# A planned attention, mix and channel kernel: gating reads removed, loads planned at another rate and later into freed buffers, one PV cost changed

## The chip, the cores and the metric

The kernel runs on one core of a Trainium2 chip. The metric is the device time of one execution in microseconds. Before the change the median of three runs is 783.98 us (780.27 to 784.87). The profile is one further execution, which took 784.69 us; its span, from the first to the last instruction, is 782.9 us.

## The reference

Three blocks follow each other, all in float32, for a batch of 4, 8 heads of 64, a sequence of 576 and a model width of 512.

```python
scores = scale * np.matmul(q, k.transpose(0, 1, 3, 2))
mask_plain = (rel >= 0) & (rel < window)                      # heads 0 to 3, window 32
mask_dil = (rel >= 0) & (rel < window * dilation) & (rel % dilation == 0)   # heads 4 to 7, dilation 4
attn = softmax(np.where(mask, scores, -1e9)); out = attn @ v

xk = mu_k * x + (1.0 - mu_k) * x_prev
xr = mu_r * x + (1.0 - mu_r) * x_prev
k = np.maximum(xk @ w_k, 0.0)
v = k * k @ w_v
r = 1.0 / (1.0 + np.exp(-(xr @ w_r)))
x = r * v

h = xt @ U @ V
u = x + h.transpose(0, 2, 1)
ch = np.maximum(u @ w_ch1, 0.0) @ w_ch2
out = u + ch
```

The weights of the second and third block reach the device as 64-bit words and are turned into float32 there.

## The kernel before

**The work.** The sequence is cut into eight half batches of 288 positions, called chunks. Attention is done for units of one pair of heads in one part of a batch; `attend` does one unit, `attend2` two units in one visit. A visit is, in order: QK products (L676, L597 for single units), masking with a row minimum on VectorE (L537, called the masks here), exponentials on ScalarE (L546), sums inverted on VectorE (L551, L552), normalisation on GpSimd (L557), transposes (L714, L628), a copy of them to SBUF on ScalarE (`pts`, L352), PV products (L732, L640). A later visit's QK stands right behind an earlier visit's PV (`join`).

Each chunk is mixed with its shifted self (`mix`, L769) and multiplied with the weights in four receptance tiles, eight key tiles and four value tiles of two parts each. Chunk 0 uses exact float32 products (L828 for the receptance rows, L812 for keys and values). The chunks 1 to 7 use two-part operands with three products (L815, L816, L817), a set of three being called a trip here. Then come the channel products in five groups (L1036 to L1038, L1113 to L1115), until the end of the kernel.

**The weights.** A piece of 512 columns of the second block's weights is loaded into one of four buffers `w64` (`cv_load`, L368), and converted by ScalarE's absolute value (L385) and four VectorE instructions (L386, L387, L389, L392) to a piece `wx`. There are 20 such pieces, w0 to w19 in this text: w0 to w3 are for the receptance rows, w4 to w7 for key tiles 0 to 3, w8 to w11 for key tiles 4 to 7, w12 to w15 for the first parts of the values, w16 to w19 for their second parts. The value tiles' first parts and second parts take 16 products each by the listing, 32 matmuls in the trace. From chunk 1 on, each `wx` is divided into two parts (L352 and L349). The third block's weights go the same way, 32 pieces, through a DRAM copy (`w2f`, L419) that is read from chunk 7 on. Attention inputs come into four buffers `raw` (L526, L530, L534).

**What sets the order.** No engine chooses at run time. Each instruction is recorded by `op` with a duration from a cost formula; `plan` runs a model of the five engines ten times (`forward`, `backward`), keeps the shortest result, and its order is the order in which each engine executes. Engines are in order, so an instruction that waits holds all that stand behind it. For SyncE, which issues every DMA, the model takes 415 ns of issue, 1300 ns, the bytes at `RATE` one transfer after another, and 700 ns. A tile that takes a buffer from an earlier one may start 40 ns after the last use that the model sees.

**The gates.** From the fifth load to the twenty-eighth, `load` records before each load a DMA of four bytes from the tile of the load four places earlier to a scratch row in DRAM (L337). It waits for that earlier load, and SyncE waits with it. There are 24. A further limit stands in the built program: DMAs take turns on eight completion semaphores, and an issue waits until the DMA eight places earlier has landed.

Of the kernel before, what the change touches and what calls it, by code (L numbers as in the profile page):

```python
# [9 lines left out]
I32 = mybir.dt.int32  # L10
# [4 lines left out]
B, H, S, D = 4, 8, 576, 64  # L15
DM, DFF, DCH, RANK = 512, 1024, 2048, 32
P = 128
# [8 lines left out]
QW, KW = 32, 64  # L26
# [5 lines left out]
NALL = len(SETS)  # L32


def unit_kind(pair, part):

    if part == 0:
        if pair < 2:
            return 10, 320, (0,) + tuple(range(0, 288, 32)), (0, 1, 1)
        return 10, 320, tuple(0 if w == 0 else 160 if w == 5 else 32 * w - 32 for w in range(10)), (2, 3, 4)  # L40
    if pair < 2:
        return 8, 288, tuple(range(0, 256, 32)), (1, 1)
    return 8, 384, tuple(96 * (w // 2) + 32 * (w % 2) for w in range(8)), (1, 1)
# [9 lines left out]
QKW, VW = 640, 640  # L53
# [13 lines left out]
SLACK = 100.0  # L67
SLACK_PE = 100.0

OUTSTANDING = 4  # L70
GATED = 28
PLAN_PRINT = None
PASSES = 10
RATE = 245.0


@with_exitstack
def tile_attention_mix_channel(
    ctx: ExitStack, tc: tile.TileContext, qk0, qk1a, qk1b, v0, v0p, v1p, cst, mu, w1raw, w2raw, upk, vpk, out
):  # L80
    nc = tc.nc
# [7 lines left out]
    cst_t = cp.tile([P, P + NALL * KW], F32, name="cst_t")  # L89
    ident = cst_t[:, 0:P]  # L90
    masks = [cst_t[:, P + i * KW : P + (i + 1) * KW] for i in range(NALL)]
    mu_t = cp.tile([P, 8], F32, name="mu_t")
# [7 lines left out]
    ops = []  # L100
# [14 lines left out]
    def bank(tag):  # L115

        return Lazy([P, 512], F32, tag, f"ps{tag}", 4, ps)
# [4 lines left out]
    def op(eng, ns, fn, r=(), w=(), more=100, lock=False, mode=None, size=0):  # L122

        o = Op()
        o.eng, o.ns, o.fn, o.r, o.w, o.more, o.lock, o.mode, o.size = eng, ns, fn, list(r), list(w), more, lock, mode, size
        ops.append(o)

    def plan():
# [28 lines left out]
        def x_end(x):  # L157
            if x.end is not None:
                return x.end
            end = 0.0  # L160
            for u in reversed(x.ops):
                if u.done is None:
                    return NEVER
                end = max(end, u.done)
            x.end = end
            return end

        def ready(o):
            t = 0.0
            for d in o.deps:  # L170
                if d.done is None:
                    return None
                t = max(t, d.done + 40)
            if getattr(o, "behind", None) and o.behind.done is None:
                return None
            for x in o.tiles:
                if x.ops[0] is not o and x.ops[0].done is None:
                    return None
            for x in o.first:
                if x.at and x.line[x.at - 1].ops[0].done is None and x.line[x.at - 1].ops[0] is not o:  # L180
                    return None
                ends = sorted((x_end(y) for y in x.line[: x.at]), reverse=True)
                if len(ends) >= x.bufs:
                    if ends[x.bufs - 1] == NEVER:
                        return None
                    t = max(t, ends[x.bufs - 1] + 40)
            return t

        def forward(rank):
# [12 lines left out]
            while len(order) < len(ops):  # L202
# [3 lines left out]
                for e, q in queues.items():  # L206
                    pick = None
                    near = []
                    for o in q:
                        if o.i > low + WINDOW:  # L210
                            break
                        near.append(o)
                    if rank is not None and e != "SP":
                        near.sort(key=lambda o: rank[o.i])
                    for o in near:
                        t = ready(o)
                        if t is None:
                            continue
                        t = max(t, free[e])
                        if o.lock:  # L220
                            t = max(t, held["POOL" if e == "DVE" else "DVE"])
                        if o.mode and mode[e] != o.mode:
                            t += 90 if e == "PE" else 1283
                        if pick is None or t < pick[0] - (SLACK_PE if e == "PE" else SLACK):
                            pick = (t, o)
                        if t <= free[e]:
                            break
                    if pick and (best is None or pick[0] < best[0]):
                        best = pick
# [5 lines left out]
                if e == "SP":  # L235
                    begin = max(t + 1300, dma)
                    dma = begin + o.size / RATE
                    o.done = dma + 700
# [46 lines left out]
    def pe(ns, fn, r, w, mode, more=300):  # L285
        if joined is not None:
            joined.append((ns, fn, r, w, mode))
            return
        op("PE", ns, fn, r, w, more, mode=mode)
# [34 lines left out]
    def dma(nbytes, fn, r, w):  # L324
        op("SP", 415, fn, r, w, size=nbytes)

    landing = []
    gate_d = tc.dram_tile([1, 64], I32, name="gate_d")

    def load(nbytes, fn, key, at):  # L330

        k = len(landing)
        landing.append((key, at))
        gate = None
        if OUTSTANDING <= k < GATED:
            seen, where = landing[k - OUTSTANDING]
            op("SP", 415, lambda: nc.sync.dma_start(gate_d[:, k : k + 1], where().bitcast(I32)[0:1, 0:1]),  # L337
               [seen], [("gate", k)], size=4)
            gate = ops[-1]
        dma(nbytes, fn, [], [key])  # L340
        ops[-1].behind = gate

    def sub(eng, n, out_, a, b, r, w, psum=False, fr=True):

# [20 lines left out]

    def cv_load(src, n):
        raw = Lazy([P, CW], I64, "w64", "w64", 4)
        load(P * n * 8, lambda: nc.sync.dma_start(raw()[:, :n], src), (raw,), lambda: raw())  # L368
        return raw

    def cv_bits(raw, n, xt_=None):
# [135 lines left out]
    def unit(u):  # L507
        part_i, pair = divmod(u, NPAIR)
        b, part = divmod(part_i, 2)
        return b, part, pair  # L510

    def a_load(u, which=("qk", "v")):
        b, part, pair = unit(u)
        nw, kc = unit_kind(pair, part)[:2]
        src = qk0[b * NPAIR + pair] if part == 0 else (qk1a if pair < 2 else qk1b)[b * 2 + pair % 2]
        alone = u < NPAIR
        at_ = 0 if alone else pair % 2 * QKW

        def tile_of(key):
            if key not in raws:  # L520
                raws[key] = Lazy([P, 2 * QKW], F32, "raw", "raw", 4)
            return raws[key]

        if "qk" in which:
            raw = tile_of(u if alone else ("qk", u // 2))
            load(P * 4 * (nw * QW + kc), lambda: nc.sync.dma_start(raw()[:, at_ : at_ + nw * QW + kc], src),  # L526
                 (raw, at_), lambda: raw()[:, at_:])
        if "v" in which and alone:
            rv = tile_of(u)
            load(P * 4 * nw * D, lambda: nc.sync.dma_start(rv()[:, QKW : QKW + nw * D], v0[u]), (rv, "v"), lambda: rv()[:, QKW:])  # L530
        elif "v" in which and pair % 2:
            vt = tile_of(("v", u // 2))
            vsrc = v0p[(b - 1) * 2 + pair // 2] if part == 0 else v1p[b * 2 + pair // 2]
            load(P * 8 * nw * D, lambda: nc.sync.dma_start(vt()[:, : 2 * nw * D], vsrc), (vt, "v"), lambda: vt())  # L534

    def low(sc, c, pr, d, mk, mn, i, r=slice(0, P)):
        nc.vector.tensor_tensor_reduce(  # L537
# [112 lines left out]
    def attend2(ua, ub):  # L650
# [5 lines left out]
        nw, kc, starts, mk = unit_kind(pair, part)  # L656
        rq, rv = raws.pop(("qk", ua // 2)), raws.pop(("v", ua // 2))
# [4 lines left out]
        pt, ov = bank("S"), [bank("S") for _ in range(2)]  # L662
        pts = Lazy([P, 5 * P], F32, "pt", "pts", 2)
# [70 lines left out]
                            rhs=pts()[r, c : c + QW], start=True, stop=True,  # L734
                        )

        pe(nw * 4 * 30, pv, [(pts, k) for k in range(nw // 2 - 3)] + [(rv, "v")], [(x,) for x in ov], "pv")
        yield
        for x in range(2):
            x_out(ov[x], pair + x, part, b)  # L740
# [420 lines left out]
    def convert_to(n):  # L1161
        nonlocal converted
        while converted < min(n, len(jobs)):
            while len(loaded) < min(converted + AHEAD, len(jobs)):
                src, k, _ = jobs[len(loaded)]
                loaded.append(cv_load(src, k))
            jobs[converted][2](loaded[converted])
            converted += 1

    def next_piece():  # L1170
        src, k, _ = jobs[len(loaded)]
        loaded.append(cv_load(src, k))

    a_load(0, ["qk"])
    load(P * 4 * (P + NALL * KW), lambda: nc.sync.dma_start(cst_t, cst), ("cst",), lambda: cst_t)
    next_piece()
    a_load(0, ["v"])
    load(P * 32, lambda: nc.sync.dma_start(mu_t, mu), ("mu",), lambda: mu_t)
    a_load(1, ["qk"])
    next_piece()  # L1180
    a_load(1, ["v"])
# [70 lines left out]
    for j in range(3):  # L1252
        at_ = (0, 5, 12)[j]
# [140 lines left out]
```

## Time and profile before

| | |
|---|---|
| median of three runs | 783.98 us |
| the profiled execution, its time | 784.69 us |
| its span | 782.9 us |
| PE busy | 740.2 us, 95% |
| PE weight loads busy | 677.0 us, 86% |
| DVE busy | 563.9 us, 72% |
| ACT, POOL busy | 394.8 us, 386.1 us |
| DMA, mean | 140 GB/s, 41.8% of 16 engines' time on the one data queue |

PE is TensorE's matmul queue, DVE VectorE, ACT ScalarE, POOL GpSimd, SP SyncE. Matmuls are pipelined, so the sum of their durations exceeds the busy time. The granted clock is 1.00 at TensorE's full 2.4 GHz. The time of the execution is 1.8 us longer than its span.

### The profile page before, as it was taken

To read this page: it belongs to the slowest core of one execution; us is meant where nothing else is said; L and a number is where in the kernel's file an instruction comes from. 1 tells how busy PE (TensorE), PEld (TensorE's weight loads), DVE (VectorE), ACT (ScalarE), POOL (GpSimd) and SP (SyncE) were. 2 spreads that over 40 slices of the span, in tenths; PEclk is the share of its full clock that TensorE was granted. 3 is DMA by queue.
4 is the path that set the end of the run, shared out by engine and by line. 5 is a ranking of instruction groups with operands and counts; after the bars stand their busy time and mean duration, and the time that the engine had idled before them with its cause. 6 is when DMAs were issued, how large, how long until landed. Compare 5 with 4: busy or idle time off the path is not lost.

```text
span 782.9 us, 18285 instructions
## 1 busy us (share of the span) xinstructions
PE 740.2 (95%) x6866; PEld 677.0 (86%) x6866; DVE 563.9 (72%) x1334; ACT 394.8 (50%) x995; POOL 386.1 (49%) x408
## 2 busy tenths in 40 slices
PE   4876998999999999999998999999999999999998
PEld 3654798899899999998998899889888999889986
DVE  4869899999989853556466879766697965665632
ACT  4567578475867674554344535443444344334310
POOL 2223225355745554436377657644587754445600
PEclk9989999999999999999999999999999999999999
DMA  7865666766785512235662244123341411132001
GB/s 247 289 207 183 199 204 199 247 224 231 236 267 175 176 45 70 91 116 167 208 207 82 87 149 164 48 81 113 131 140 55 136 53 64 47 109 81 28 1 54
DMA packets 53273, 109.78 MB, mean 140 GB/s; under 512 B 5697, under 2 KB 15937, under 8 KB 53185
## 3 DMA queue, kind: packets, MB, share of 16 engines
q1 hardware_dynamic: 53184, 108.62, 41.8%
q8 instruction: 54, 0.88, 0.5%
q14 instruction: 35, 0.28, 0.1%
HBM read 86.05 MB, written 22.54 MB: 139 GB/s over the span
## 4 chain that ended last, share of the span: by engine, by line
PE 73%; DVE 13%; DMA 4%; issue 3%; ACT 3%; POOL 2%; SPq 0%; DVEq 0%; POOLq 0%; ACTq 0%
PE psS L1115 8%; PE psS L1113 8%; PE psS L1114 8%; PE psM L1036 7%; PE psM L1038 7%; PE psM L1037 7%; PE psM L815 7%; PE psM L816 6%; PE psM L817 6%; PE psS L732 2%; PE psS L676 1%; PE psM L812 1%; DVE pr L537 1%; DVE sums L472 1%; PE psM L828 1%
## 5 line engine op out<-in xcount | busy, mean ns | idle before, releaser
L347 POOL TENSOR_TENSOR cl<-sums,ch 128x512 fp32r<-128x512 f32 x72 | 98.3, 1366 | 89.2 <-ACT ch L352 60.0
L1115 PE MATMUL psS<-hl,rh 128*128 128x512 f32 (+1 forms) x320 | 119.8, 375 | 1.6 <-DVE hl L1051 1.6
L1113 PE MATMUL psS<-hh,rh 128*128 128x512 f32 (+1 forms) x320 | 119.3, 373 | 0.9 <-ACT hh L1050 0.5
L1114 PE MATMUL psS<-hh,rl 128*128 128x512 f32 (+1 forms) x320 | 119.1, 372 | 0.9 <-DVE rl L349 0.9
L352 ACT ACTIVATE ch<-sums 128x512 fp32r<-128x512 f32 (+1 forms) x104 | 57.3, 561 | 102.9 <-DVE sums L472 95.3
L815 PE MATMUL psM<-xk,wh 128*128 128x288 f32 x336 | 101.9, 303 | 0.0
L816 PE MATMUL psM<-xk,wl 128*128 128x288 f32 x336 | 99.8, 297 | 0.2 <-DVE wl L349 0.2
L817 PE MATMUL psM<-xk,wh 128*128 128x288 f32 x336 | 99.4, 296 | 0.0
L347 POOL TENSOR_TENSOR cl<-st,ch 128x256 fp32r<-128x256 f32 x80 | 65.5, 836 | 56.0 <-PE psM L1038 32.3
L472 DVE TENSOR_TENSOR sums<-st 128x256 f32<-128x256 f32 (+1 forms) x144 | 86.5, 651 | 5.0 <-POOL cl L347 3.8
L347 POOL TENSOR_TENSOR k2s<-k,k2s 128x288 fp32r<-128x288 f32 x49 | 46.5, 948 | 58.1 <-ACT k2s L352 56.3
L1115 PEld LDWEIGHTS psS<-hl,rh 128*128 128x128 f32 x320 | 60.5, 189 | 13.6 <-DVE hl L1051 2.0
L1113 PEld LDWEIGHTS psS<-hh,rh 128*128 128x128 f32 x320 | 60.5, 189 | 11.2 <-ACT hh L1092 1.2
L1114 PEld LDWEIGHTS psS<-hh,rl 128*128 128x128 f32 x320 | 60.5, 189 | 10.6 <-DVE rl L349 1.1
L347 POOL TENSOR_TENSOR xk<-m,xk 128x288 fp32r<-128x288 f32 x56 | 51.7, 936 | 36.2 <-ACT xk L352 30.5
L815 PE MATMUL psM<-k2s,wh 128*128 128x288 f32 x224 | 67.1, 300 | 0.0
L816 PE MATMUL psM<-k2s,wl 128*128 128x288 f32 x224 | 66.1, 295 | 0.7 <-issue 0.7
L817 PE MATMUL psM<-k2s,wh 128*128 128x288 f32 x224 | 65.9, 294 | 0.0
L815 PEld LDWEIGHTS psM<-xk,wh 128*128 128x128 f32 x336 | 63.7, 189 | 0.9 <-DVE y L877 0.3
L816 PEld LDWEIGHTS psM<-xk,wl 128*128 128x128 f32 x336 | 63.7, 190 | 0.5 <-DVE wl L349 0.5
L817 PEld LDWEIGHTS psM<-xk,wh 128*128 128x128 f32 x336 | 63.8, 190 | 0.0
L1093 DVE SCALAR_TENSOR_TENSOR hl<-ort,hh 128x512 fp32r<-128x512 f32 x32 | 26.8, 836 | 50.1 <-ACT hh L1092 49.1
(147 smaller groups left out, 2129.7 us busy)
## 6 DMA issues: line engine op xcount, KB each, us to landing
st<-w2f SPq DMA_DIRECT2D x96, 256.0 KB, 3.1
w<-w2raw SPq DMA_DIRECT2D x32, 512.0 KB, 5.7
w<-w1raw SPq DMA_DIRECT2D x20, 512.0 KB, 4.5
w2f<-w SPq DMA_DIRECT2D x32, 256.0 KB, 2.3
raw<-qk SPq DMA_DIRECT2D x16, 320.0 KB, 6.3
ytmp<-y SPq DMA_DIRECT2D x32, 144.0 KB, 3.3
yb<-ytmp SPq DMA_DIRECT2D x4, 1152.0 KB
uf<-us SPq DMA_DIRECT2D x32, 144.0 KB, 1.8
```

Of the source, the lines that this page charges most:

```text
L347: op("POOL", t, lambda: nc.gpsimd.tensor_tensor(out=out_(), in0=a(), in1=b(), op=ALU.subtract), r, w, 40, lock=True)
L352: act(n, lambda: nc.scalar.activation(out_(), in_(), AF.Copy), r, w, psum, strided)
L472: dve(k * Q, lambda: nc.vector.tensor_tensor(out=q(sm_, n, k)(), in0=a(), in1=b(), op=op_), [(s1,), (s2,)], [(sm_, key)], two=True)
L815: nc.tensor.matmul(a, lhsT=wh, rhs=xh, start=start, stop=False)
L816: nc.tensor.matmul(a, lhsT=wl, rhs=xh, start=False, stop=False)
L817: nc.tensor.matmul(a, lhsT=wh, rhs=xl, start=False, stop=stop)
L1036: nc.tensor.matmul(a, lhsT=wh()[:, wi], rhs=xh()[:, ci], start=(k == 0), stop=False)
L1037: nc.tensor.matmul(a, lhsT=wl()[:, wi], rhs=xh()[:, ci], start=False, stop=False)
L1038: nc.tensor.matmul(a, lhsT=wh()[:, wi], rhs=xl()[:, ci], start=False, stop=(k == len(parts) - 1))
L1113: nc.tensor.matmul(a, lhsT=wh, rhs=xh, start=(j == 0 and e == 0), stop=False)
L1114: nc.tensor.matmul(a, lhsT=wl, rhs=xh, start=False, stop=False)
L1115: nc.tensor.matmul(a, lhsT=wh, rhs=xl, start=False, stop=(j == 7 and e == 1))
```

## The change

Five edits. The gates go, with the table that they needed, and loads are recorded without a predecessor. `RATE`, at which the model moves bytes, goes from 245 to 285 GB/s. A new constant `LATE` makes the model wait 1500 ns instead of 40 before a DMA may be issued into a buffer that was used before. The PV products of `attend2` are planned at 34 ns instead of 30. No compute instruction is added or removed.

```diff
-OUTSTANDING = 4
-GATED = 28
+LATE = 1500.0
-RATE = 245.0
+RATE = 285.0
...
-            if getattr(o, "behind", None) and o.behind.done is None:
-                return None
...
-                    t = max(t, ends[x.bufs - 1] + 40)
+                    t = max(t, ends[x.bufs - 1] + (LATE if o.eng == "SP" else 40))
...
-    landing = []
-    gate_d = tc.dram_tile([1, 64], I32, name="gate_d")
-
-    def load(nbytes, fn, key, at):
-
-        k = len(landing)
-        landing.append((key, at))
-        gate = None
-        if OUTSTANDING <= k < GATED:
-            seen, where = landing[k - OUTSTANDING]
-            op("SP", 415, lambda: nc.sync.dma_start(gate_d[:, k : k + 1], where().bitcast(I32)[0:1, 0:1]),
-               [seen], [("gate", k)], size=4)
-            gate = ops[-1]
+    def load(nbytes, fn, key):
+
         dma(nbytes, fn, [], [key])
-        ops[-1].behind = gate
...
-        pe(nw * 4 * 30, pv, [(pts, k) for k in range(nw // 2 - 3)] + [(rv, "v")], [(x,) for x in ov], "pv")
+        pe(nw * 4 * 34, pv, [(pts, k) for k in range(nw // 2 - 3)] + [(rv, "v")], [(x,) for x in ov], "pv")
```

All five engines get another order. Lines behind the edits stand 15 lower in the changed kernel (L812 becomes L797), those in `forward` and shortly behind 3 lower.

SyncE, loads of weight pieces and attention inputs shortly after the start, before and then after; `w64_223` and `w64_132` are w2, `w64_278` and `w64_145` w3.

```order
L337 DMA gate_d_90<-w64_144 1x1
L368 DMA w64_223<-w1raw 128x512
L337 DMA gate_d_90<-raw_135 1x1
L526 DMA raw_235<-qk0 128x640
L337 DMA gate_d_90<-raw_156 1x1
L530 DMA raw_235<-v0 128x640
L337 DMA gate_d_90<-raw_156 1x1
L368 DMA w64_278<-w1raw 128x512
```

```order
L353 DMA w64_132<-w1raw 128x512
L511 DMA raw_142<-qk0 128x640
L515 DMA raw_142<-v0 128x640
L353 DMA w64_145<-w1raw 128x512
L511 DMA raw_258<-qk1a 128x544
L353 DMA w64_261<-w1raw 128x512
```

The same loads stand in the same succession, with no four-byte read between them.

VectorE, from the reciprocal of unit 3 on, before and then after; `wx_380` and `wx_352` are w3, `wx_429` and `wx_411` w4, `wx_456` w5, `wx_471` w6, and the L769 row with `d_427` is the first mix of the third pair of heads, which the third receptance row needs.

```order
L552 RECIPROCAL sm_406<-sm_406 128x5
L392 SCALAR_TENSOR_TENSOR wx_380<-w64_278,wx_380 128x512
L386 TENSOR_SCALAR wx_429<-wx_429 128x512
L769 SCALAR_TENSOR_TENSOR xk0_284<-d_427,mu_t_87,x0_94 128x288
L387 TENSOR_SCALAR wx_429<-wx_429 128x512
```

```order
L537 RECIPROCAL sm_397<-sm_397 128x5
L371 TENSOR_SCALAR wx_411<-wx_411 128x512
L372 TENSOR_SCALAR wx_411<-wx_411 128x512
L371 TENSOR_SCALAR wx_456<-wx_456 128x512
L374 SCALAR_TENSOR_TENSOR wx_411<-w64_261,wx_411 128x512
L372 TENSOR_SCALAR wx_456<-wx_456 128x512
L377 SCALAR_TENSOR_TENSOR wx_411<-w64_261,wx_411 128x512
L371 TENSOR_SCALAR wx_471<-wx_471 128x512
L374 SCALAR_TENSOR_TENSOR wx_456<-w64_291,wx_456 128x512
L372 TENSOR_SCALAR wx_471<-wx_471 128x512
L377 SCALAR_TENSOR_TENSOR wx_456<-w64_291,wx_456 128x512
```

Ten conversion instructions, and behind them eight masks and two more, now stand before that mix, where two stood.

VectorE, the last rows before the masks of the second visit (`L537 ISA pr_656` before, `L522 ISA pr_653` after): before w6 is the last piece there, after w8 (`wx_573` is w6, `wx_543` w7, `wx_566` w8).

```order
L386 TENSOR_SCALAR wx_573<-wx_573 128x512
L387 TENSOR_SCALAR wx_573<-wx_573 128x512
L389 SCALAR_TENSOR_TENSOR wx_573<-w64_536,wx_573 128x512
L392 SCALAR_TENSOR_TENSOR wx_573<-w64_536,wx_573 128x512
L537 ISA pr_656,mn_657<-psS_611,cst_t_86 128x64
```

```order
L371 TENSOR_SCALAR wx_543<-wx_543 128x512
L754 SCALAR_TENSOR_TENSOR xk0_274<-d_461,mu_t_87,x0_93 128x288
L372 TENSOR_SCALAR wx_543<-wx_543 128x512
L374 SCALAR_TENSOR_TENSOR wx_543<-w64_459,wx_543 128x512
L377 SCALAR_TENSOR_TENSOR wx_543<-w64_459,wx_543 128x512
L371 TENSOR_SCALAR wx_566<-wx_566 128x512
L372 TENSOR_SCALAR wx_566<-wx_566 128x512
L374 SCALAR_TENSOR_TENSOR wx_566<-w64_503,wx_566 128x512
L377 SCALAR_TENSOR_TENSOR wx_566<-w64_503,wx_566 128x512
L522 ISA pr_653,mn_654<-psS_604,cst_t_86 128x64
```

So the pieces for key tiles 0 to 3 end ahead of that visit's masks and not behind them. In the same way w11 moves from behind the next visit's twelve masks to ahead of them, and w16 to w19 from behind the masks of the visit after that to ahead of them.

PE, the end of chunk 0, before and then after; `k_733` and `k_725` are the squared keys, the operand of the value products.

```order
L812 MATMUL psM<-xk_284,wx 128x288 x16
L714 MATMUL psS<-cst_t,pr 128x128 x5
L732 MATMUL psS<-pts,raw 64x32 x40
L676 MATMUL psS<-raw 32x64 x40
L812 MATMUL psM<-k_733,wx 128x288 x32
L714 MATMUL psS<-cst_t,pr 128x128 x5
```

```order
L797 MATMUL psM<-xk_274,wx 128x288 x16
L797 MATMUL psM<-k_725,wx 128x288 x16
L699 MATMUL psS<-cst_t,pr 128x128 x5
L717 MATMUL psS<-pts,raw 64x32 x40
L661 MATMUL psS<-raw 32x64 x40
L797 MATMUL psM<-k_725,wx 128x288 x16
L699 MATMUL psS<-cst_t,pr 128x128 x5
```

Half of the value products moves ahead of the visit that stood before all of them.

## Rows read from the trace of the kernel before

**Rows 1.** Busy time by stretch: length, busy us (instructions) of each engine, clock, DMA share, GB/s

```profile
core 0: us, PE busy (x) PEld busy (x) DVE busy (x) ACT busy (x) POOL busy (x), PEclk, DMA share, GB/s
0.00:30.00 30.00, 18.20 (x370) 14.00 (x371) 17.35 (x78) 14.00 (x52) 6.79 (x16) 1.00 0.78 260
30.00:60.00 30.00, 22.81 (x328) 16.90 (x329) 22.07 (x72) 20.73 (x63) 7.71 (x10) 0.83 0.68 224
60.00:90.00 30.00, 22.07 (x287) 16.84 (x274) 28.42 (x95) 21.62 (x71) 10.29 (x12) 0.89 0.56 182
...
98.00:140.00 42.00, 37.83 (x401) 36.39 (x400) 40.25 (x93) 30.91 (x72) 17.70 (x18) 0.98 0.62 203
140.00:260.00 120.00, 118.33 (x1773) 115.83 (x1772) 113.25 (x340) 82.38 (x255) 64.63 (x74) 0.99 0.70 230
260.00:320.00 60.00, 60.00 (x749) 58.88 (x748) 31.45 (x102) 36.38 (x106) 31.06 (x41) 1.00 0.23 74
320.00:440.00 120.00, 114.65 (x871) 110.51 (x870) 74.16 (x128) 54.35 (x111) 63.58 (x61) 0.99 0.46 151
```

**Rows 2.** What PE waited for, 0 to 98 us: total us, times, longest

```profile
PE psM L812 <- DVE wx L392: 8.6, 2, 4.5
PE psS L732 <- ACT pts L352: 4.5, 2, 3.5
PE psM L828 <- DVE xk L769: 0.9, 1, 0.9
```

**Rows 3.** What PE waited for, 98 us to the end

```profile
PE psS L714 <- POOL pr L557: 3.9, 2, 3.2
```

**Rows 4.** Timeline of PE: start, us, instruction xcount [idle before it <- what ended it]

```profile
30.33 2.14 PE L828 MATMUL psM<-xk,wx 128*128 128x288 f32 x8
...
75.04 0.71 PE L714 MATMUL psS<-cst_t,pr 128*128 128x128 f32 x5
79.23 1.37 PE L732 MATMUL psS<-pts,raw 64*64 64x32 f32 x80 [3.47 <-ACT pts L352]
...
82.02 16.72 PE L812 MATMUL psM<-k,wx 128*128 128x288 f32 x64
98.57 0.71 PE L714 MATMUL psS<-cst_t,pr 128*128 128x128 f32 x5
...
138.68 0.69 PE L714 MATMUL psS<-cst_t,pr 128*128 128x128 f32 x2 [3.21 <-POOL pr L557]
```

**Rows 5.** What DVE waited for, 0 to 90 us: total us, times, longest

```profile
DVE wx L386 <- ACT wx L385: 9.0, 5, 5.2
DVE pr L537 <- PE psS L597: 7.7, 4, 4.6
DVE pr L537 <- PE psS L676: 2.3, 2, 1.7
```

**Rows 6.** Timeline of DVE

```profile
59.11 0.43 DVE L386 TENSOR_SCALAR wx<-wx 128x512 f32<-128x512 f32 x1 [5.17 <-ACT wx L385]
...
62.52 0.21 DVE L537 CUSTOM_DVE_ANT_0 pr<-psS,cst_t 128x64 f32<-128x64 f32 x1
...
64.43 0.23 DVE L537 CUSTOM_DVE_ANT_0 pr<-psS,cst_t 64x64 f32<-64x64 f32 x1
...
90.49 0.65 DVE L392 SCALAR_TENSOR_TENSOR wx<-w,wx 128x512 int32<-128x512 int32 x1
```

**Rows 7.** Busy time by stretch, near the start: the last two numbers are DMA share and GB/s

```profile
2.00:7.00 5.00, 0.91 (x40) 0.67 (x40) 1.36 (x14) 1.79 (x11) 0.00 (x0) 1.00 0.92 312
7.00:9.00 2.00, 0.00 (x0) 0.00 (x0) 0.67 (x3) 0.66 (x1) 1.01 (x2) 1.00 0.23 88
9.00:14.00 5.00, 4.08 (x83) 3.38 (x83) 4.29 (x19) 2.79 (x12) 0.00 (x0) 1.00 0.97 326
```

**Rows 8.** Timeline of SP's queue: issue of DMAs, start and us

```profile
1.67 0.42 SPq L368 DMA_DIRECT2D w<-w1raw  x1
...
7.64 0.25 SPq L337 DMA_DIRECT2D gate_d<-w  x1
```

**Rows 9.** One line's instructions, L392: duration ns min/median/max

```profile
L392 DVE SCALAR_TENSOR_TENSOR wx<-w,wx x20: 651/686/1276, 11.4 to 90.5; 128x512 int32<-128x512 int32 x20
```

More of the change, by code (lines that the diff above doesn't have):

```diff
@@ L367, in cv_load @@
         raw = Lazy([P, CW], I64, "w64", "w64", 4)
-        load(P * n * 8, lambda: nc.sync.dma_start(raw()[:, :n], src), (raw,), lambda: raw())
+        load(P * n * 8, lambda: nc.sync.dma_start(raw()[:, :n], src), (raw,))
         return raw
@@ L526, in a_load @@
             load(P * 4 * (nw * QW + kc), lambda: nc.sync.dma_start(raw()[:, at_ : at_ + nw * QW + kc], src),
-                 (raw, at_), lambda: raw()[:, at_:])
+                 (raw, at_))
         if "v" in which and alone:
             rv = tile_of(u)
-            load(P * 4 * nw * D, lambda: nc.sync.dma_start(rv()[:, QKW : QKW + nw * D], v0[u]), (rv, "v"), lambda: rv()[:, QKW:])
+            load(P * 4 * nw * D, lambda: nc.sync.dma_start(rv()[:, QKW : QKW + nw * D], v0[u]), (rv, "v"))
         elif "v" in which and pair % 2:
@@ L533, in a_load @@
             vsrc = v0p[(b - 1) * 2 + pair // 2] if part == 0 else v1p[b * 2 + pair // 2]
-            load(P * 8 * nw * D, lambda: nc.sync.dma_start(vt()[:, : 2 * nw * D], vsrc), (vt, "v"), lambda: vt())
+            load(P * 8 * nw * D, lambda: nc.sync.dma_start(vt()[:, : 2 * nw * D], vsrc), (vt, "v"))
     def low(sc, c, pr, d, mk, mn, i, r=slice(0, P)):
@@ L1174, in tile_attention_mix_channel @@
     a_load(0, ["qk"])
-    load(P * 4 * (P + NALL * KW), lambda: nc.sync.dma_start(cst_t, cst), ("cst",), lambda: cst_t)
+    load(P * 4 * (P + NALL * KW), lambda: nc.sync.dma_start(cst_t, cst), ("cst",))
     next_piece()
     a_load(0, ["v"])
-    load(P * 32, lambda: nc.sync.dma_start(mu_t, mu), ("mu",), lambda: mu_t)
+    load(P * 32, lambda: nc.sync.dma_start(mu_t, mu), ("mu",))
     a_load(1, ["qk"])
```

## The prediction

> **What bounds the kernel now.** I read the busy time by stretch first. From 98 us on PE is busy nearly all the time (118.33 of 120 us between 140 and 260, 60.00 of 60 behind that), so there the end can move only by its small idle rests; in the first 90 us it is busy 63.08 of 90 at a granted clock of 0.83 to 1.00 [rows 1]. What a planner's change can win lies at the start. Next come PE's waits there: key tiles that wait for a converted weight piece (8.6 us in two waits), PV that waits for the copied transposes (4.5 in two) [rows 2]. Last, why the weights are late: VectorE itself is idle 22 of its first 90 us, and 9.0 of them it waits for ScalarE's absolute value, longest 5.17, which stands in ScalarE's order behind copies that wait for PE [rows 5, 6]. So PE waits for VectorE, VectorE for ScalarE and ScalarE for PE; the order closes this ring, and only the order can open it. Behind 98 us one wait stands out, transposes on the normalised probabilities, 3.21 us [rows 3, 4].
>
> **Part one: the gates.** 24 four-byte DMAs go, 0.25 us of SyncE's issue each by the row shown, 6 us in all [rows 8]. SyncE is not on the path for that; what counts is what it holds back. With gates the DMA engines moved 312 GB/s from 2 to 7 us and 326 from 9 to 14, but 88 from 7 to 9, while SyncE waited at 7.64 for the first weight piece [rows 7, 8]. So the queue fills even with four loads under way, except for such holes. The second unit's inputs stand at the same place in the queue, behind the same bytes: no gain for the first 9 us. Later pieces land earlier by the hole, some 1.5 us (2 us at 326 less 88, over 326). I book this inside part two.
>
> Do the early loads land later when eight are under way and not four? The first weight piece was issued at 1.67 and landed at 7.64, when the gate on it went out, 5.97 us with three other large loads beside it [rows 8]. The Trainium skill, DMA: Bandwidth & Descriptors, section Queues, rings and completion order, says that each of the sixteen engines takes the descriptors of a queue in ring order; by that rule a load issued behind cannot take from one ahead, and the sum keeps a zero. If loads shared the rate evenly instead, the second unit's inputs would land with the last of the eight, up to 1.5 us later by the hole just priced, and the sum would be 1.5 us longer.
>
> **Part two: the order of chunk 0, from the planner's rate.** In the new order w7 and w8 are converted ahead of the second visit's masks, w11 ahead of the third's, and w16 to w19 ahead of the fourth's. That is where the ring was: key tiles 0 to 3 and 4 to 7 need w7 and w11, and found them behind masks that wait for PE's own QK.
>
> I count VectorE up to the end of w19's conversion, 91.1 us before [rows 6]. It was busy 17.35 + 22.07 + 28.42 us to 90 and all the time behind that, 68.9 us, and so idle 22.2 [rows 1]. In the new order twelve masks go behind w19: from 62.52 to 64.66, 2.1 us [rows 6]. Of the idle time 7.7 us for the first units' QK stays, it is the attention's own latency, and so does the 2.3 for the visits' QK; of the 9.0 for ScalarE I let 7.5 go (the 5.17, and all else but 1.5 for the very first piece, before which no load can have landed) [rows 5]. Then w19 is ready at 68.9 - 2.1 + 22.2 - 7.5 = 81.5 us.
>
> PE needs more than that. Its value products were 64 matmuls in 16.72 us, 0.261 each [rows 4]. Now 32 of them stand ahead of a visit and 32 behind it. The first half's first tile uses w15 only in its last product of four, two matmuls each, so 6 of the 32 matmuls can be done before w15 is ready and 26 stand behind it: the half ends at w15 + 26 x 0.261 = w15 + 6.8. Between w15 and w19 VectorE has sixteen conversion instructions (0.69 us for the dearer half, whose median is shown, and 0.43 for the others, as at 59.11, hence 9.0), three mixes and two pairs of reciprocals, to which I give 1.5 us: 10.5, from which I take a tenth because such instructions overlap at their ends, so 9.4 [rows 6, 9]. So w15 is ready at 72.1 and the half ends at 78.9. The visit between the halves took 82.02 - 75.04 = 6.98 us before, 3.47 of it one wait for the copy; the other such wait was 1.0 (4.5 less 3.5), and I take that one: 4.5 us [rows 2, 4]. The second half runs from 83.4 to 91.8 us. Before, it ended where the next transposes began, 98.57 [rows 4]. Gain: 6.8 us. Its bounds: 98.57 less (81.5 + 6.8), 10.3 us, if w19 alone decides, and zero if the ring closes at another place.
>
> The same order costs something. The mix for the third receptance row now stands behind ten conversion instructions and eight masks; that row began at 30.33 before [rows 4]. Ten instructions of about 0.5 us and two more behind the masks move it to about 36 or 37, and PE will wait there some 5 us where it waited less than 0.9 [rows 2]. VectorE works through it, so in the count above this costs nothing: PE's loss is bought back when the key tiles run without a wait.
>
> **Part three: after chunk 0.** The wait of 3.21 us stood in a visit with 24 trips between its QK and its transposes [rows 4]; the new order puts 48 trips there, twice the work, so nothing is left to wait for. Gain 3.2. But it makes 24 trips of the distance in three later visits, where there were 28 or more. Each could cost what the one did: 0 to 9.6 us; the row of that visit shows the masks late by VectorE's other work, which the planner has moved, so I take half of one wait, 1.6 us lost.
>
> **Part four: LATE, and the price of PV.** LATE moves loads later in SyncE's order, mostly the re-reads of `w2f` from 320 us on. PE is idle 5.35 of 120 us there [rows 1]. Bounds: all of it gained, or as much again lost; I take zero. The PV price issues nothing and removes nothing; it pushes transposes and PV apart by a trip or two in the model. The wait that it can touch is the 4.5 us in rows 2, already used. Zero.
>
> **Sum.** 784.69 - 6.8 - 3.2 + 1.6 = 776.3 us against the profiled execution, which stood 0.7 above the median of 783.98; so 775.6, and I say 776.
>
> **The rivals.** *Handed back.* VectorE is busy 40.25 of 42 us from 98 to 140 and 113.25 of 120 from there to 260: if PE arrives seven us early, VectorE cannot follow, and PE's lead shrinks to the 8.5 us of idle time that VectorE has there, less what it already uses [rows 1]. Against it: the third block's conversions, most of that work, are first read from chunk 7 on, and from 260 to 320 VectorE has 28.5 us free; in the new order about three pieces fewer are converted when the first key tile of chunk 1 is done, which is just the lead. If it decides, only the 3.2 and a us or two of the lead remain: 780. The Trainium skill, SBUF — State Buffer, section SECX, states that VectorE and GpSimd exclude each other from a shared port pair for a whole instruction; the row agrees in that L392 took 1276 ns at worst and 686 in the middle [rows 9]. By that rule a denser start makes each conversion dearer; with 25 us of GpSimd work in 90, a tenth of it met would take 2.5 us from the gain [rows 1].
>
> *The change does not do what it says.* The gates held back only the one hole, since 326 GB/s flowed with them [rows 7], and the waits reappear at the third receptance row and the second visit. For it: 5 us of new waiting there by my own count. Against it: VectorE's 5.17 us goes, whatever PE does. Time: 783.
>
> *Slower: loads land late.* With eight in flight a piece may take twice the time. ScalarE's absolute values of w4 to w8 now stand ahead of the copies that PE waits for, and SyncE issues w7 behind inputs that wait for unit 2's PV and w8 behind those that wait for unit 3's. If a piece took 9 us and not the 6 of the first one, three rounds of four buffers pass on 3 us each, 9 us, and nothing of part two is left: 784 + 9 = 793. It decides from about 8 us for a load. Against it: the rate was full with four, so bytes ahead in the queue, not sharing, set the landing.
>
> **How the numbers follow.** One per cent, 7.8 us, is about what a measurement of this kernel can tell from no change. My forecast has a chance of 0.55, with 769 to 781 as its own range; the bound at 776.1 cuts it nearly in half, 0.30 above 1% and 0.25 within. A better outcome, where w19 alone decides (10.3 us) and PE's rests from 320 us on shrink too, has 0.15 and ends near 768. Handed back has 0.10, no effect 0.07, slower 0.13 (0.11 of it beyond 1%). So faster 0.45, same 0.44, slower 0.11. The range reaches from 767, the better case, to 788, half way to the slower one, which leaves out about two in ten.
>
> **What would show it.** Right: no wait of key tiles on L392's counterpart over 1 us, VectorE's wait on ScalarE under 2 us in the first 90, the first two-part product of chunk 1 at about 92 us and not 99, no 3 us wait at the transposes near 130. PE should wait some 5 us before the third receptance row. Wrong: if chunk 1 begins at 92 and the end does not move, it was handed back; if a weight load takes over 8 us to land and PE idles more than 27 us in the first 90, it is the slower rival.

## The result and the profile after

The changed kernel takes 773.31 us in the median of five executions (772.45 to 775.42) beside 782.12 us of the kernel before in the same comparison (778.76 to 785.18): ratio 0.9892, 95% interval 0.9852 to 0.9932. A sixth execution was slow, 4007.15 us, and stands in none of these numbers. The forecast was 776, range 767 to 788. The profiled execution took 774.71 us, its span is 772.5 us against 782.9.

Line numbers have moved: L582, L661, L699, L717, L797, L813 are now QK, QK, transposes, PV, key and value products and receptance rows (L597, L676, L714, L732, L812, L828 before); L371, L377, L337 and L370 stand for L386, L392, L352 and L385.

Busy time by stretch of the changed kernel, columns as in [rows 1] and [rows 7]:

```profile
0.00:30.00 30.00, 18.65 (x412) 14.74 (x412) 19.42 (x83) 15.65 (x55) 7.42 (x16) 1.00 0.86 293
30.00:60.00 30.00, 21.50 (x334) 16.54 (x331) 24.29 (x88) 20.35 (x63) 9.66 (x12) 0.85 0.72 246
60.00:90.00 30.00, 27.42 (x251) 21.11 (x250) 24.56 (x81) 19.06 (x66) 7.23 (x10) 0.87 0.48 152
...
98.00:140.00 42.00, 41.08 (x450) 40.62 (x445) 40.96 (x111) 28.28 (x79) 20.36 (x25) 1.00 0.62 209
...
320.00:440.00 120.00, 115.91 (x881) 112.33 (x880) 79.49 (x133) 54.31 (x114) 67.50 (x65) 0.99 0.47 150
...
9.00:14.00 5.00, 4.39 (x107) 3.51 (x90) 4.32 (x20) 3.45 (x14) 0.30 (x1) 1.00 1.03 393
```

PE is busy 67.57 us of the first 90 instead of 63.08, and 41.08 of 42 from 98 to 140 instead of 37.83; from 320 to 440 it gains little, 115.91 beside 114.65 [rows 1]. The last line answers to one of [rows 7]: the same five microseconds moved 326 GB/s before, 393 now.

Some of what PE waited for in the changed kernel, first 0 to 98 us, then 98 us to the end (total us, times, longest). "Issue" is time in which the engine waited for nothing that the profile names. Left out are the waits for the first attention inputs, 8.6 us before and 7.6 now:

```profile
PE psM L813 <- DVE xk L754: 4.6, 1, 4.6
PE psS L661 <- issue: 3.3, 1, 3.3
PE psS L699 <- POOL pr L542: 1.7, 1, 1.7
PE psS L717 <- ACT pts L337: 1.5, 2, 0.9
...
PE psS L1099 <- DVE rl L334: 2.8, 1, 2.8
PE psS L717 <- ACT pts L337: 2.5, 2, 1.6
...
PE psS L699 <- POOL pr L542: 0.6, 1, 0.6
```

VectorE's wait for ScalarE, of the first 90 us, answers to the first line of [rows 5]:

```profile
DVE wx L371 <- ACT wx L370: 4.5, 4, 2.1
```

The 8.6 us of the key tiles and the 4.5 of PV in [rows 2] have gone or shrunk; the third receptance row waits 4.6 where it waited 0.9. Behind 98 us the wait of 3.2 in [rows 3] has gone; a wait of 2.8 on `rl`, the low part of a row of the channel mix's second weight, is new.

PE's timeline of the changed kernel, for [rows 4]:

```profile
34.66 4.21 PE L813 MATMUL psM<-xk,wx 128*128 128x288 f32 x8 [4.55 <-DVE xk L754]
...
43.90 8.03 PE L797 MATMUL psM<-xk,wx 128*128 128x288 f32 x32
...
58.34 0.64 PE L661 MATMUL psS<-raw 64*32 64x64 f32 x14 [3.26 <-issue]
58.91 10.72 PE L797 MATMUL psM<-xk,wx 128*128 128x288 f32 x32
69.47 8.03 PE L797 MATMUL psM<-k,wx 128*128 128x288 f32 x32
77.34 0.38 PE L699 MATMUL psS<-cst_t,pr 128*128 128x128 f32 x2
79.45 0.55 PE L699 MATMUL psS<-cst_t,pr 128*128 128x128 f32 x3 [1.73 <-POOL pr L542]
...
84.16 8.36 PE L797 MATMUL psM<-k,wx 128*128 128x288 f32 x32
92.36 0.73 PE L699 MATMUL psS<-cst_t,pr 128*128 128x128 f32 x5
92.85 0.38 PE L800 MATMUL psM<-xk,wh 128*128 128x288 f32 x1
```

Chunk 0 ends at 92.36 where it ended at 98.57: 6.2 us.

A wait of PE cost more here than its own length. The stop of 3.26 us before 58.34 is followed by a granted clock of 0.50, TensorE's lower level of 1.2 GHz (column before the last two):

```profile
58.34:64.00 5.66, 5.66 (x25) 4.06 (x26) 3.44 (x27) 0.81 (x3) 0.15 (x1) 0.50 0.71 244
```

So the 32 matmuls at 58.91 take 10.72 us where the 32 at 43.90, at 1.00, take 8.03: 2.7 us more. The eight behind the wait of 4.55 take 4.21 where the next eight, at 39.51, take 2.60. The kernel before paid the same way behind its two waits for weight pieces:

```profile
47.95 9.16 PE L812 MATMUL psM<-xk,wx 128*128 128x288 f32 x26 [4.17 <-DVE wx L392]
67.06 8.15 PE L812 MATMUL psM<-xk,wx 128*128 128x288 f32 x26 [4.45 <-DVE wx L392]
```

At 8.03 us for 32, 26 take 6.5, so the clock added 2.6 and 1.6 us.

The rest of this document reads every kernel in three stretches, from its own trace, which is one execution. Executions of one kernel differ by up to ten microseconds (e3: 771.79 to 781.65), so a difference of one or two between stretches of two kernels shows nothing by itself; the ratios rest on all executions. *Start* is the time of the first two-part product of chunk 1 (99.0 before, 92.9 after); *middle* goes from there to the first product of the channel mix's first layer (L1036 before, L1021 now; 373.4 and 364.0); *mix* is all behind that, to the end of the span. The row of that product in the changed kernel, first and last start behind the durations:

```profile
L1021 PE MATMUL psM<-tr,ch x192: 276/280/415, 364.0 to 748.3; 128*128 128x256 f32 x192
```

Where a planner moves a visit across a mark, start and middle shift against each other, so their sum is safer than either.

| kernel (RATE, LATE, PV) | ratio, 95% | start | middle | mix |
|---|---|---|---|---|
| before: reads planned and issued (245, 40, 30) | 1 | 99.0 | 274.4 | 409.5 |
| changed: no reads (285, 1500, 34) | 0.9892, 0.9852–0.9932 | 92.9 | 271.1 | 408.5 |
| e1: order of before, reads not issued | 0.996, 0.9932–0.9988 | 96.5 | 274.6 | 407.5 |
| e2: order of the changed kernel, reads issued | 0.9908, 0.9872–0.9943 | 97.4 | 270.1 | 409.5 |
| e3: no reads (245, 40, 30) | 0.9928, 0.9891–0.9965 | 92.8 | 274.0 | 407.4 |
| e4: reads planned, issued (285, 1500, 34) | 0.9812, 0.9757–0.9867 | 92.0 | 270.7 | 407.8 |
| e5: e4's order, reads not issued | 0.9847, 0.9816–0.9877 | 89.5 | 270.3 | 409.2 |
| e6: no reads (245, 1500, 34) | 0.9863, 0.9826–0.9900 | 98.1 | 264.6 | 406.8 |
| e7: no reads (285, 40, 34) | 0.9802, 0.9760–0.9844 | 90.0 | 272.5 | 401.9 |
| e8: no reads (285, 1500, 30) | 0.9839, 0.9788–0.9890 | 91.8 | 269.2 | 409.3 |
| e9: as changed, LATE not on `st` | 0.9800, 0.9748–0.9851 | 92.0 | 272.6 | 402.6 |
| e10: as changed, LATE on `st` alone | 0.9832, 0.9799–0.9866 | 90.2 | 274.0 | 405.0 |
| e11: no reads (245, 40, 34) | 1.0001, 0.9976–1.0025 | 95.8 | 277.4 | 408.4 |
| e12: no reads (285, 40, 30) | 0.9809, 0.9769–0.9848 | 84.5 | 280.1 | 403.5 |

So of the 10.4 us that the span lost, 6.2 lie in the start, 3.2 in the middle and 1.0 in the mix.

### The profile page after: what moved, and what is told of

It is laid out like the page before. It is cut to its first block, busy times and chain, and to the rows that moved or that the text cites. A ratio compares the mean times of both kernels' runs of the same rounds, so it can differ in the third digit from the quotient of the medians.

```text
span 772.5 us, 18230 instructions
## 1 busy us (share of the span) xinstructions
PE 735.6 (95%) x6866; PEld 675.2 (87%) x6866; DVE 569.0 (74%) x1334; ACT 391.4 (51%) x995; POOL 388.1 (50%) x408
## 5 line engine op out<-in xcount | busy, mean ns | idle before, releaser
L337 ACT ACTIVATE ch<-sums 128x512 fp32r<-128x512 f32 (+1 forms) x104 | 57.3, 561 | 104.6 <-DVE sums L457 98.9
L332 POOL TENSOR_TENSOR cl<-st,ch 128x256 fp32r<-128x256 f32 x80 | 67.2, 855 | 55.3 <-PE psM L1023 35.1
L1058 DVE TENSOR_TENSOR ok<-ok,psM 128x256 f32<-128x256 f32 (+1 forms) x96 | 46.4, 504 | 21.0 <-PE psM L1023 18.7
```

The costliest lines, as they stand in the source:

```text
L332: op("POOL", t, lambda: nc.gpsimd.tensor_tensor(out=out_(), in0=a(), in1=b(), op=ALU.subtract), r, w, 40, lock=True)
L337: act(n, lambda: nc.scalar.activation(out_(), in_(), AF.Copy), r, w, psum, strided)
L1058: dve(k * Q, lambda: nc.vector.tensor_tensor(out=out_(), in0=a(), in1=b(), op=op_), r, w, two=True, psum=True)
```

## The experiments

**The reads by themselves: e1, e2, e3.** e1 is the kernel before with its order kept and its reads not sent:

```diff
-            op("SP", 415, lambda: nc.sync.dma_start(gate_d[:, k : k + 1], where().bitcast(I32)[0:1, 0:1]),
+            op("SP", 415, lambda: None,
```

e2 is the changed kernel with a read sent ahead of each of the fifth to the twenty-eighth load, unknown to the planner:

```diff
+        def both():
+            if where is not None:
+                nc.sync.dma_start(gate_d[:, k : k + 1], where().bitcast(I32)[0:1, 0:1])
+            fn()
-        dma(nbytes, fn, [], [key])
+        dma(nbytes, both, [], [key])
```

e3 is the changed kernel with the three old numbers (`RATE = 245.0`, `LATE = 40.0`, PV 30), so that the reads alone are gone, from program and plan.

> The order of the kernel before, instruction for instruction, but the 24 four-byte reads are not issued. Theory (the gain is in the planner's order): the ring of VectorE, ScalarE and PE stays, key tiles still wait over 3 us twice for L392, chunk 1 begins at 97 to 99 us, time within 3 us of the kernel before. Rival (the reads held the loads back, and that was the cost): the waits on L392 fall under 1 us each and the time is 6 us or more below the kernel before.

> The order of the changed kernel, but each of the fifth to twenty-eighth load is preceded by the four-byte read of the load four places earlier. Theory: chunk 1 begins at 92 to 95 us and the time is 1 to 3 us above the changed kernel, for the hole of 1.5 us that the first reads leave in the transfers. Rival: chunk 1 begins at 97 us or later and the time is within 2 us of the kernel before.

> The reads dropped from the program and from the planner's model; rate 245, 40 ns and 30 ns as before. Theory: the planner, freed of the reads, already finds the loads earlier and puts w7 ahead of the second visit's masks, so most of the gain at the start comes, 3 to 7 us below the kernel before. Rival (the rate of 285 is what makes the order): within 2 us of the kernel before.

Measured: 781.05 us beside 783.68 for e1, 778.26 for e2, 779.61 for e3 (ratios in the table). Not sending the reads brings the start 2.5 us forward in the old order (99.0 to 96.5) and 4.5 in the new one (97.4 to 92.9). The data rate fits; stretch 9 to 14 us of e1, then of e2, last column:

```profile
9.00:14.00 5.00, 3.93 (x83) 3.36 (x83) 4.34 (x18) 2.72 (x12) 0.00 (x0) 1.00 1.03 407
```

```profile
9.00:14.00 5.00, 4.08 (x83) 3.37 (x83) 3.30 (x18) 2.66 (x12) 0.00 (x0) 1.00 0.91 303
```

With the reads 303 GB/s here and 326 before, without them 407 here and 393 in the changed kernel; e4 and e5 below, one order with and without, moved 306 and 405. Four loads under way did not fill the queue. At the end e1 keeps 0.4% of it, and the changed kernel's interval and e2's overlap by far more than they differ. For e1 that is its theory but for a start half a microsecond earlier than said: its two waits for weight pieces are still 4.2 and 4.5 us. e2 met neither of its expectations whole: its start, 97.4, is the rival's, its time, 5.4 us below the kernel before, is not. e3 is 4.1 us below the kernel before, as its theory said, and starts as early as the changed kernel (92.8), though one wait of the old ring is still there:

```profile
PE psM L797 <- DVE wx L377: 5.5, 2, 5.2
```

So the start did not need the new numbers; the planner's new order without the reads gives 92.8 at the old rate too.

**The numbers by themselves: e4, e5.** e4 leaves the reads in plan and program and sets only `RATE = 285.0`, LATE 1500 and PV 34; e5 is e4 with the edit of e1.

> The kernel before with rate 285, 1500 ns and 34 ns, the reads kept in model and program. Theory: SyncE still waits at the reads in the model, so the order of the start stays near the old one, 0 to 4 us below the kernel before. Rival (the rate makes the order): 6 us or more below.

> The order of e4 (the planner reckons with the four-byte reads, and with RATE 285, LATE 1500, PV 34), but the reads are not issued. Theory: the reads cost 2.5 to 4 us on the chip in any order (e1 against the kernel before, e2 against the changed kernel), so the ratio to before is 0.976 to 0.979, 767 to 769 us. Rival: in this order the reads hide behind loads that have time to spare, so the time is that of e4, ratio 0.981, 771 to 772 us.

Measured: e4 771.88 us, ratio 0.9812; e5 770.74, ratio 0.9847. e4's theory fell: it is 11.8 us below the kernel before, its rival's outcome. With the reads kept, the numbers alone make at least the gain of the changed kernel, which drops the reads and sets the numbers; e4's ratio is the lower one, with intervals that just overlap. e5's theory, 0.976 to 0.979, is outside its interval: the start came 2.5 us forward once more, 92.0 to 89.5, the middle stayed and the mix gave 1.4 back; no gain over e4 can be measured. A lead at the start is not a lead at the end.

**Each number taken back: e6, e7, e8.** The changed kernel with one of its three numbers at the old value, one line of these for each kernel.

```diff
-RATE = 285.0
+RATE = 245.0
...
-LATE = 1500.0
+LATE = 40.0
...
-        pe(nw * 4 * 34, pv,
+        pe(nw * 4 * 30, pv,
```

> The changed kernel with RATE back at 245; LATE and PV stay. Theory (the rate carries the gain of the new numbers): the time goes back to that of e3, ratio 0.993, 778 to 780 us, and the third receptance row waits less than 2 us, as in e3. Rival (no number carries it; the planner's order scatters with any of them): 2 to 6 us away from the changed kernel in either direction, and another order of the later chunks decides.

> The changed kernel with LATE back at 40. Theory (the rate carries the gain, LATE is worth nothing, as forecast): within 2 us of the changed kernel, ratio 0.987 to 0.991, and the start up to 92 us as in it. Rival (scatter): 2 to 6 us away, the difference after 92 us.

> The changed kernel with PV back at 30. Theory (PV is worth nothing, as forecast): within 2 us of the changed kernel, ratio 0.987 to 0.991. Rival (scatter): 2 to 6 us away.

Measured: 772.04, 766.28 and 771.51 us beside 782.73. No number carries the gain alone: with any one of them back the ratio is lower than the changed kernel's, for e7 with its whole interval, for e6 and e8 with intervals that overlap. The theory that the rate carries the gain falls with e6, though the third receptance row waits there as little as in e3 (1.0 us at the longest); "LATE is worth nothing" falls with e7. e8 does not settle its question, since its interval reaches into its theory's range.

**Where LATE costs.** In the mix e7 is 6.6 us shorter than the changed kernel. Changed kernel, SyncE's queue, ScalarE, VectorE and PE around the new wait, and two stretches:

```profile
367.76 0.53 SPq L954 DMA_DIRECT2D ug<-uf  x1
368.38 0.59 SPq L430 DMA_DIRECT2D st<-w2f  x1
369.02 9.52 SPq L937 DMA_DIRECT2D uf<-us  x3
```

```profile
376.46 1.15 ACT L337 ACTIVATE tA<-ug 128x512 fp32r<-128x512 f32 x2 [6.20 <-DMA ug<-uf]
377.52 0.61 ACT L337 ACTIVATE rh<-st 128x512 fp32r<-128x512 f32 x1
378.04 1.14 ACT L337 ACTIVATE tA<-tmp 128x512 fp32r<-128x512 f32 x2
379.08 0.62 ACT L337 ACTIVATE rh<-st 128x512 fp32r<-128x512 f32 x1
```

```profile
379.44 1.78 DVE L1003 TENSOR_TENSOR tmp<-ug 128x512 f32<-128x512 f32 x1
381.14 0.68 DVE L1036 SCALAR_TENSOR_TENSOR hl<-psM,hh 128x512 fp32r<-128x512 f32 x1
381.74 2.36 DVE L457 TENSOR_TENSOR sums<-st 128x256 f32<-128x256 f32 x2
...
386.88 4.06 DVE L334 TENSOR_TENSOR rl<-st,rh 128x512 fp32r<-128x512 f32 x3
```

```profile
388.16 0.39 PE L1099 MATMUL psS<-hh,rl 128*128 128x256 f32 x1 [2.82 <-DVE rl L334]
```

```profile
380.00:390.00 10.00, 7.18 (x56) 6.98 (x55) 10.00 (x10) 4.93 (x11) 10.00 (x8) 0.93 0.51 167
390.00:400.00 10.00, 10.00 (x79) 10.00 (x78) 4.29 (x7) 3.69 (x8) 3.50 (x4) 0.90 0.78 242
```

The same in e7, SyncE, ScalarE, VectorE:

```profile
366.23 0.32 SPq L430 DMA_DIRECT2D st<-w2f  x1
367.10 0.52 SPq L954 DMA_DIRECT2D ug<-uf  x1
```

```profile
368.82 1.15 ACT L337 ACTIVATE rh<-st 128x512 fp32r<-128x512 f32 x2
373.54 1.16 ACT L337 ACTIVATE tA<-ug 128x512 fp32r<-128x512 f32 x2 [3.57 <-DMA ug<-uf]
```

```profile
369.49 1.29 DVE L334 TENSOR_TENSOR rl<-st,rh 128x512 fp32r<-128x512 f32 x2
```

In the changed kernel a load of `st` goes out behind the read of `ug`, in e7 ahead of it. ScalarE's `rh`, made from `st`, then stands behind `tA`, made from `ug`, and ScalarE waits 6.20 us for `ug`; VectorE's eighth `rl` ends up behind `tmp`, `hl` and the sums and is made at 386.88 instead of 370.1. PE waits 2.82 us, and its granted clock is 0.93 and 0.90 in the two stretches in which e7 has 1.00: an estimated 10 x 0.07 + 10 x 0.10 = 1.7 us more. Together 4.5 of the 6.6; the rest is not accounted for.

**LATE on part of the loads, and in other company: e9 to e12.** e9 spares the loads into `st`, which are all 96 re-reads of `w2f` and not those of one weight alone, e10 (`== "st"`) spares all others; e11 has LATE and RATE back, e12 LATE and PV.

```diff
-                    t = max(t, ends[x.bufs - 1] + (LATE if o.eng == "SP" else 40))
+                    t = max(t, ends[x.bufs - 1] + (LATE if o.eng == "SP" and x.args[2] != "st" else 40))
```

> The changed kernel, but LATE holds only for loads other than those of the second weight into the tile st (st stays at 40). Theory (LATE's cost sits at 388 us: two st loads were planned behind a store on the SyncE queue that waits for us, so rl came late, PE waited 2.8 us and its clock fell after it): no wait of 2 us on rl after 350 us, granted clock 1.00 from 370 to 400 us, ratio 0.979 to 0.984, 766 to 770 us. Rival (the wait is taken up by others, e7 was a good order by chance): the wait goes and the end moves by less than 2 us, ratio 0.987 to 0.991.

> The changed kernel, but LATE holds only for the loads into st; all others are at 40, as in e7. Theory: the wait of PE on rl, 2.8 us, is back and the granted clock falls below 0.95 after it, so 4 to 5 us over e9: ratio 0.985 to 0.990, 770 to 775 us. Rival: the time of e7, ratio 0.980.

> The changed kernel with LATE at 40 and RATE at 245, so PV 34 alone is new beside the dropped reads. Theory: e6 (LATE 1500 at this rate) had no wait of PE on rl, so LATE is worth little here: within 2 us of e6, ratio 0.984 to 0.989. Rival (LATE costs 5 us or more at either rate): ratio 0.977 to 0.981.

> The changed kernel with LATE at 40 and PV at 30, so RATE 285 alone is new beside the dropped reads. Theory: e8 (LATE 1500) had the wait of 2.8 us on rl; without LATE it goes, 4 to 6 us under e8: ratio 0.976 to 0.980. Rival (the orders scatter and e7 was a good one by chance): within 2 us of e8, ratio 0.982 to 0.986.

Measured beside 784.6: e9 769.29, e10 770.99, e11 784.26, e12 769.76 us. e9 answers as its theory did: no wait on `rl`, `rh` ahead of `tA` again, the clock at 1.00, the mix 5.9 us shorter. ScalarE, then the two stretches, of e9:

```profile
373.26 1.15 ACT L337 ACTIVATE rh<-st 128x512 fp32r<-128x512 f32 x2 [2.44 <-DMA st<-w2f]
376.89 1.15 ACT L337 ACTIVATE tA<-ug 128x512 fp32r<-128x512 f32 x2 [2.48 <-DMA ug<-uf]
```

```profile
380.00:390.00 10.00, 10.00 (x88) 10.00 (x86) 8.79 (x9) 5.78 (x12) 10.00 (x8) 1.00 0.47 157
390.00:400.00 10.00, 10.00 (x87) 10.00 (x86) 7.32 (x12) 5.00 (x10) 5.60 (x7) 1.00 0.85 265
```

In one thing the expectation was wrong. It blamed two `st` loads behind the `uf<-us` store that holds SyncE for 9.52 us; by the rows above it was the one load ahead of that store, behind `ug`.

e10 misses its main point: its mix is 2.4 us longer than e9's, but the wait on `rl` did not return. PE waited 1.9 us on `us` at 378.25, ahead of that place, and so may have met `rl` later. So LATE on `st` alone does not bring the wait:

```profile
PE psS L1098 <- DVE us L934: 1.9, 1, 1.9
```

e11 met neither of its expectations: no gain at all. Its start of 95.8 is given back in the middle, 277.4, with this wait among others behind 92 us:

```profile
PE psS L717 <- ACT pts L337: 3.5, 2, 2.5
```

e12 lies between its two expectations and its interval does not part them; the wait on `rl` is gone and the mix 5.8 us shorter than e8's, as the theory said. But its start, the earliest of all, was handed back in the middle, by PV waiting between 84 and 365 us:

```profile
PE psS L717 <- ACT pts L337: 7.9, 5, 3.0
```

Read in pairs that differ in one number: in the mix LATE costs 6.6 (e7 to the changed kernel) and 5.8 us (e12 to e8) at RATE 285, and gains 1.6 at 245 (e11 to e6); RATE gains 3.9 (e3 to e12) and 6.5 (e11 to e7) at LATE 40, and costs 1.7 at LATE 1500 (e6 to the changed kernel). Start and middle follow no such rule. PV 34 costs 7.4 us of span at (245, 40), e3 to e11, and 0.7% or 5.7 us by the ratios; at (285, 40) the span is 3.7 us shorter with it and at (285, 1500) 2.2 longer, both with overlapping intervals.

## Why the prediction was right, and where it was not

**What bounds the kernel** held: 9.4 of 10.4 us came ahead of the channel mix, 6.2 of them in the start. But the clock of 0.83 to 1.00 that was read there got no term in the sum.

**Part one, the gates.** "So the queue fills even with four loads under way" was the step that failed. 326 GB/s was what four loads reach, and not what the queue can do: 393 to 409 without the reads. The reads were booked at 1.5 us inside part two; not sending them moves the start by 2.5 to 4.5. "No gain for the first 9 us" was wrong too: QK of the second unit began at 8.48 us and not 9.33, 0.85 earlier. That early loads do not land later held: the first weight piece, issued at 1.66 us, was in use at 6.68 with eight loads issued behind it by then, where it was 7.64 with three. That agrees with the rule of the Trainium skill (DMA: Bandwidth & Descriptors, Queues, rings and completion order) that each DMA engine takes a queue's descriptors in ring order.

**Part two, chunk 0.** 91.8 was forecast for its end, 92.36 measured. Of its own terms: the first half of the value products ended at 77.3 (forecast 78.9), the visit between the halves took 84.16 - 77.34 = 6.8 us and not 4.5, the second half 8.4 as said. w15 was ready at 70.9 (forecast 72.1), just as PE came to it, and w19 at 85.0 (81.5), since VectorE still waited 4.5 us for ScalarE where under 2 was forecast and 3.0 for the QK that PE stopped in. The third receptance row waited 4.55 (forecast 5), and no key tile waited for a weight piece. That the end agrees within 0.6 us is partly luck. PE lost 3.3 us in the middle of a QK, which nothing in the trace before announced, and 2.7 more by the clock behind it, 6.0 in all; against that stand the reads, worth more than booked, and the 4.2 us that the clock had cost behind the two old waits. No run parts these. And the cause was put too narrowly. The planner's rate opens the ring, but e3 starts at 92.8 with the old rate and half the ring still closed.

VectorE's row for the second such line, L377, stands beside [rows 9]:

```profile
L377 DVE SCALAR_TENSOR_TENSOR wx<-w,wx x20: 652/684/1172, 11.7 to 83.9; 128x512 int32<-128x512 int32 x20
```

684 ns in the middle and 1172 at worst, 686 and 1276 before: the dearer conversions that the Trainium skill's rule on the shared port pair would bring (SBUF — State Buffer, section Who interferes with whom, which is the section meant above) did not come.

**Part three.** The wait of 3.2 us went. In its place stand 2.5 on copied transposes and 0.6 on probabilities, 1.6 at the longest; the middle gained 3.2 us, where 1.6 net was forecast.

**Part four, LATE and PV at zero,** was right in sum by luck. In the mix the changed kernel gained 1.0 us. Step by step that is 2.1 from the reads (before to e3), 3.9 from the rate (to e12), which was not priced there at all, 5.8 lost by LATE (to e8) and 0.8 from PV; by another way the rate gave 6.5 and LATE took 6.6. "I take zero" hid two terms of more than half the forecast gain each. Against e7 LATE costs 0.9% of the time, 7 us, more than the bound of 5.35. PV's zero has no clear answer at LATE 1500, and is wrong at (245, 40).

**The rivals.** Handed back did not happen in the changed kernel, whose middle is shorter too; it did in e12 and e11, where 84.5 and 95.8 at the start became 364.6 and 373.2 at the mix. Slower by late landing is excluded: a weight piece took 4.9 us in the median from issue to landing, 4.5 before, where that rival needed about 8. Where the gain sits e1 and e2 show between them: the new order with the reads still sent has 0.9908, the old order without them 0.996. So the forecast number came true with a mis-sized term of the reads, no term for the clock or the stop, and a zero that was two terms.

The best kernel here is e7, the change without LATE: 766.28 us, ratio 0.9802; e9, with LATE kept off `st`, is not to be told from it, nor are e12, with the rate alone, and e4, which keeps the reads: removing them is not needed for the gain. Not settled: what LATE does alone, since no run has (245, 1500, 30), why PV 34 undoes all the gain at (245, 40), and how much of the spread of start and middle is a planner that reacts to small numbers in no regular way. No run took the PE stall or the third row's wait away by itself.

## What to carry to other kernels

A group of planner numbers is to be tested one at a time and by stage: here, with the reads dropped, any two of three gave at least the gain of all three, one alone (the rate, e12) gave 1.9% and another (PV, e11) nothing, and LATE and the rate, each a gain over e11 by itself (0.9863 and 0.9802), gave no more together (0.9892). Where a load is moved, follow the engine that converts it: 1.5 us of delay in the plan cost an estimated 4.5 on the chip, since a conversion fell behind one that waits for a slow transfer. Price a wait of TensorE with the clock that follows it. A data rate seen under a limit on loads in flight is not the ceiling, and a lead at the start counts only when the next stage's waits are read too.

## What the hardware showed that was not expected

The DMA engines moved 393 to 409 GB/s from 9 to 14 us without the four-byte reads (the changed kernel, e1, e3, e5), 303 to 326 with them (before, e2, e4).

PE stopped 1.1 to 3.8 us within a QK between 53 and 63 us in ten of the kernels with a new order, waiting for nothing that the profile names, each time at the 1451st to 1454th of its instructions. In the changed kernel the stop lasts from 55.1 to 58.34. DMA queues of that kernel, 55.9 to 57 us:

```profile
q8 instruction: 1, 0.02, 5.5%
```

A block of 16 KB on the instruction queue lies inside the stop, from 55.99 to 56.95. There are 54 such blocks in the span, 0.88 MB, about 64 bytes for each of PE's 13,732 instructions; the profile does not say for which engine a block is. In all ten kernels PE went on 1.1 to 1.5 us after such a block had passed. In the four that did not stop (before, e1, e3, e12), PE came to this instruction 1.4 us or more after such a block. That PE ran out of code while the loads had the engines is the reading that fits; no run here shows it by itself. The earliest start, e12's 84.5, is in a kernel without the stop.
